# Gate sums of four chunks as triangular matmuls, clamp replaced by row sums, a first chunk in halves and constant matmuls, in a gated linear attention with a token-mixing block

## The chip, the cores and the metric

The kernel runs on one core of one Trainium2 chip. The metric is the device time of one execution in microseconds (us), the median of several runs: 340.54 us before, from 339.99 to 340.63 in three runs.

## The reference

Two stages, all in float32. The first is a recurrence over 768 tokens for 4 batches of 8 heads, with 48 values a head:

```
f = 1 / (1 + exp(-f_logit))
for t in range(S):
    state = f[:, :, t, :, None] * state + outer(k[:, :, t], v[:, :, t])
    y[:, :, t] = q[:, :, t] @ state
```

The second takes y as x with 384 channels a token:

```
theta = x @ w_theta
y = w_tok_r @ (x * cos(theta)) + w_tok_i @ (x * sin(theta))
u = x + y
out = u + maximum(u @ w_ch, 0)
```

## The kernel before, in words

The 768 tokens of a batch are cut into six chunks of 128, 24 chunks in all (m from 0 to 23). The eight heads lie as four pairs on the 128 partitions, so that a tile of q, k or f is 128 x 4 x 128, 256 KB.

*Gates of a chunk.* `gate_clamp` (L234) holds f at -44 or above, on VectorE or POOL. `gate_open` (L238) takes Exp and Ln on ScalarE, which gives minus the log of the gate. `gate_sum` (L244) sums it along the chunk's tokens with a scan on VectorE, where the constant tile carry begins each pair anew. `gate_exp` (L248) takes Exp of the negative sum into tile p, of which there is one buffer, and Exp of the sum in place of f. `gate_q` (L259) multiplies q by p, `gate_k` (L263) k by the held f tile. `gate_end` (L256) keeps the last column of p in `pes` on POOL.

*Attention of a chunk.* `att_keys` transposes k into psk, `att_ktok` copies it out, `att_state` (L314) forms k times v for both halves of the chunk, `att_scores` and `att_mask` (L300) the scores under the causal mask, `att_mid`, `att_new` and `att_fade` the state, `att_old` and `att_out` (L360) y, which `att_x` copies to x. v comes with a second copy whose heads are rolled.

*The second stage.* x is transposed (pxt) into ut; `angles` (L396) multiplies by w_theta into pth; `whole`, `settle`, `fold`, `trig` and `rotate` (L428) turn it into z = x cos, x sin; `products` (L447) sums z with the token weights over six chunks into pm; `add_u`, `split_uh`, `split_ul`, `channel` (pch) and `finish` do the rest. Batch 0 does this in float32; the later batches split each operand in a high and a low part in fp32r (`split_xh`, `split_xl`, `split_zh`, `split_zl`, `split_uh`, `split_ul`). The weights come as 64-bit floats; `decode_low`, `decode_high` and `decode_join` turn them into float32 (the steps d1, d2, d3), part by part: the parts 0 and 1 are w_theta, the next 12 the token weights.

*Order.* Nothing schedules the work but `ORDER` (L53): a list of steps, done from left to right, that puts each step's instructions behind the earlier ones of the same engine (L569). A letter after a slash moves the step to another engine (A ScalarE, D VectorE, P POOL). All loads and stores stand in one queue, SP's. A step is a name such as `gs` (gate_sum), `ge` (gate_exp), `gk`, `gq`, `ke` (att_keys), `up` (att_state) or `f0` (products for one third of the channels), and its n-th occurrence does the n-th chunk or piece.

*End.* `find_worst` (L500) makes a flag from `pes`; if it is set, a slow recurrence runs instead (it does not here). The last 128 x 3 x 384 tile is stored at L650, after the branch.

PSUM has two rings: two double banks "a", and four banks "b" for psk, pxt, pth, pm and pch.

Of the kernel before, what the change touches and what calls it, by code (L numbers as in the profile page):

```python
# [698 lines left out]
```

## Time and profile before

| | |
|---|---|
| median of 3 runs | 340.54 us |
| profiled execution | 340.03 us |
| its span, first to last instruction | 338.3 us |
| TensorE (PE) busy | 320.4 us, 95% |
| VectorE (DVE) busy | 251.6 us, 74% |
| ScalarE (ACT) busy | 188.7 us, 56% |
| POOL busy | 108.6 us, 32% |
| moved | 45.5 MB, 135 GB/s |

A busy share is that of the whole span, an average over stages that differ. PE is the matmuls and PEld the weight loads, which overlap them; the ends of matmuls are modelled. An f32 matmul shows as two records, a transpose as one. What matters is where an engine waits, and for whom.

### The profile page before, as it was taken

Reading aid. Unit: us, or ns where it says so; the run is one execution under the profiler, and the core shown is the slowest. Engines: PE = TensorE matmul, PEld = TensorE weight load, DVE = VectorE, ACT = ScalarE, POOL = GpSimd, SP = SyncE. Lnnn points to the kernel's source line nnn. Section 1 sums busy time; section 2 is a strip of 40 time slices with the busy share of each in tenths; the row PEclk is TensorE's granted clock in tenths of the full one; section 3 lists DMA queues with packets and bytes.
Section 4 is the critical chain, followed back from the end, with each engine's and each line's share of the span. In section 5 each row is a group of like instructions: output and inputs, shape, how many; then the busy total and the mean of one; then the engine's idle time right before and its main releaser. Section 6 shows DMA issues by size and latency. Waiting matters only on the chain. (4 is left out here: it accounts for less than half of the span.)

```text
span 338.3 us, 9998 instructions
## 1 busy us (share of the span) xinstructions
PE 320.4 (95%) x4320; PEld 283.2 (84%) x4320; DVE 251.6 (74%) x411; ACT 188.7 (56%) x308; POOL 108.6 (32%) x105
## 2 busy tenths in 40 slices
PE   0789999999999999999999999999999999999993
PEld 0676766776776789999999999999999999999992
DVE  5989999999999998898987857855437848534211
ACT  6787997995866755588476685244076114400010
POOL 3585152134418235701445423323212201300010
PEclk9999999999999999999999999999999999999998
DMA  7994994738761262374124320532121120000012
GB/s 256 382 401 168 317 372 151 249 114 323 244 224 30 64 230 82 91 233 141 33 85 149 122 79 2 187 114 84 40 73 48 47 73 27 0 2 0 11 60 78
DMA packets 21618, 45.54 MB, mean 135 GB/s; under 512 B 2368, under 2 KB 5440, under 8 KB 21568
## 3 DMA queue, kind: packets, MB, share of 16 engines
q1 hardware_dynamic: 21568, 44.84, 38.5%
q8 instruction: 36, 0.59, 0.7%
q14 instruction: 14, 0.11, 0.1%
HBM read 40.11 MB, written 4.72 MB: 133 GB/s over the span
## 5 line engine op out<-in xcount | busy, mean ns | idle before, releaser
L458 PE MATMUL pm<-wp,z 128*128 128x384 f32 x648 | 118.4, 337 | 0.0
L458 PEld LDWEIGHTS pm<-wp,z 128*128 128x128 f32 x648 | 112.4, 188 | 0.4
L458 PE MATMUL pm<-value,z 128*128 128x384 f32 x144 | 49.3, 487 | 0.0
L476 PE MATMUL pch<-uhl,wch 128*128 128x384 f32 x216 | 40.0, 337 | 0.0
L458 PEld LDWEIGHTS pm<-value,z 128*128 128x128 f32 x144 | 26.4, 190 | 15.2
L476 PEld LDWEIGHTS pch<-uhl,wch 128*128 128x128 f32 x216 | 37.4, 188 | 0.0
L469 POOL TENSOR_TENSOR uhl<-ut,uhl 128x384 fp32r<-128x384 f32 x13 | 14.2, 1094 | 67.0 <-ACT uhl L143 35.5
L236 POOL TENSOR_SCALAR f<-f 128x512 f32<-128x512 f32 x16 | 26.6, 1666 | 13.3 <-DMA f<-in_f_dram 12.5
L246 DVE TENSOR_TENSOR_SCAN f<-carry,f 128x512 f32<-128x512 f32 x24 | 29.8, 1246 | 1.4 <-ACT f L242 1.4
L257 POOL COPY pes<-p 128x4 f32<-128x4 f32 x24 | 10.5, 439 | 52.9 <-ACT p L253 52.9
L490 DVE SCALAR_TENSOR_TENSOR ut<-pch,ut 128x384 f32<-128x384 f32 x24 | 13.1, 550 | 18.8 <-PE pch L476 17.1
L308 PE MATMUL psk<-ident,k 128*128 128x128 f32 x96 | 16.9, 303 | 10.0 <-DVE k L266 10.0
L261 POOL TENSOR_TENSOR q<-q,p 128x512 f32<-128x512 f32 x12 | 17.3, 1446 | 23.1 <-ACT p L253 14.6
L462 DVE TENSOR_TENSOR ut<-pm,ut 128x384 f32<-128x384 f32 x24 | 13.0, 551 | 14.2 <-PE pm L458 14.2
L253 ACT ACTIVATE p<-f 128x512 f32<-128x512 f32 x24 | 15.1, 630 | 14.4 <-DVE f L246 6.8
L402 PE MATMUL pth<-wth,xh 128*128 128x384 f32 x108 | 23.0, 348 | 0.0
L308 PEld LDWEIGHTS psk<-ident,k 128*128 128x128 f32 x96 | 12.2, 153 | 12.3 <-issue 10.3
L435 DVE TENSOR_TENSOR w<-w,x 128x768 f32<-128x768 f32 x18 | 17.2, 962 | 6.3 <-ACT w L426 6.3
L143 ACT COPY x<-py 128x384 f32<-128x384 f32 x19 | 9.1, 478 | 22.5 <-PE py L361 22.1
L361 PEld LDWEIGHTS py<-v,sc 64*64 64x64 f32 x768 | 15.0, 140 | 7.4 <-issue 4.5
L143 ACT CAST uhl<-ut 128x384 fp32r<-128x384 f32 x7 | 3.6, 513 | 31.1 <-DVE ut L462 17.5
L266 DVE SCALAR_TENSOR_TENSOR k<-f,k 128x512 f32<-128x512 f32 x24 | 18.2, 758 | 1.8 <-ACT f L254 1.1
(83 smaller groups left out, 622.6 us busy)
## 6 DMA issues: line engine op xcount, KB each, us to landing
v<-in_v_dram SPq DMA_DIRECT2D x24, 384.0 KB, 4.3
f<-in_f_dram SPq DMA_DIRECT2D x24, 256.0 KB, 3.8
q<-in_q_dram SPq DMA_DIRECT2D x24, 256.0 KB, 4.1
k<-in_k_dram SPq DMA_DIRECT2D x24, 256.0 KB, 4.3
raw<-in_w_r_dram SPq DMA_DIRECT2D x12, 384.0 KB, 5.9
raw<-in_w_i_dram SPq DMA_DIRECT2D x12, 384.0 KB, 6.3
out_dram<-ut SPq DMA_DIRECT2D x21, 192.0 KB, 1.9
raw<-in_w_theta_dram SPq DMA_DIRECT2D x3, 384.0 KB, 6.4
```

The costliest lines, as they stand in the source:

```text
L236: on(nc.vector).tensor_scalar(ft, ft, F_MIN, None, op0=ALU.max)
L246: nc.vector.tensor_tensor_scan(fl, carry[:, pairs(h)].rearrange("p n t -> p (n t)"), fl, 0.0, ALU.mult, ALU.add)
L253: nc.scalar.activation(ps_[m][:, pairs(h)], ft, AF.Exp, scale=-1.0)
L261: on(nc.vector).tensor_tensor(qt, qt, ps_[m][:, pairs(h)], op=ALU.mult)
L266: nc.vector.scalar_tensor_tensor(kt, loaded["f", m][:, pairs(h)], E_TOP, kt, op0=ALU.min, op1=ALU.mult)
L308: nc.tensor.transpose(psks[m][:, p, :], loaded["k", m][:, p, :], ident)
L361: nc.tensor.matmul(out[HALF[t], j, p, :], scs[m][HALF[a], j, p, :], v2[HALF[a], t, p, :], start=(t == 0 and m % NC == 0 and p == 0), stop= ...
L402: nc.tensor.matmul(pths[m], l, r, start=(n == 0), stop=(n == len(ms) - 1))
L435: nc.vector.tensor_tensor(zs[m] if full else w, w, xs[m].unsqueeze(1).to_broadcast([P, 2, DM]), op=ALU.mult)
L458: nc.tensor.matmul(pms[g, d], l, r, start=(s == 0 and i == 0), stop=(s == NC - 1 and i == len(ms) - 1))
L469: on(nc.vector).tensor_tensor(us[g, d][:, 0], uts[g][:, d, :], us[g, d][:, 1], op=ALU.subtract)
L476: nc.tensor.matmul(pcs[g, d], l, r, start=(es[0] == 0 and n == 0), stop=(es[-1] == KD - 1 and n == len(ms) - 1))
```

## The change

- **The clamp goes.** `gate_open` writes, with its first Exp, the sum of each row into a column of `opened`; `find_worst` raises the flag where such a sum is above 1e18, too.
- **v** is loaded as three tiles of 192 columns instead of two of 384: 288 KB a chunk for 384.
- **Halves.** `CUT` is 1: chunk 0's loads and gates (f, k, q) are done in two halves of two pairs (the steps `hlf`, `hgo`, `hgs` and so on).
- **Sums as matmuls.** For the first four chunks (`SUMMED`) f is loaded with the tokens on the partitions (`ft`), and `gate_sum` is four f32 matmuls of 128x128 with the triangular tile `upto` into a bank of ring "b" instead of a scan. `gate_exp` reads that bank.
- **p and f change roles.** p holds Exp of the sum and meets k; the f tile holds Exp of its negative and meets q and `pes`.
- **Constant matmuls.** `keep_warm` (`wu`) multiplies the identity by a part of carry, into a bank nobody reads; there are 30.
- **New order.** `decode_high` can also be done on VectorE or POOL.

```diff
-CUT = 0
+CUT = 1
+SUMMED = 4
...
 ORDER = (
-    "lf gc lf gc go go gs lf gc/P lq lk lv gs ge gq gp go ge gk lw lk gs ke kt up gp sc lq gq/P d1 lw lq d2 gk ke",
+    "hlf wu wu wu hgo lf go lf go hlf hgo wu wu wu wu wu wu hgs lk wu wu wu gs gs ge wu lw hlq gk hgs hge hge d1",
+    "hlk hgk hgq/P wu hlq wu wu wu wu gp hlk hgk ke ke hgq d2 d3 lv kt ge up sc sa gp st sm/P lk kt lw d1 lv d2/P",
...
-    "f2 f2 ul so f2 cv cv c cv uh ul/P f2 v uh c c ul/P so c so so so rv cv cv cv",
+    "f2 f2 v uh ul/P f0 f0 uh/D ul c cv f1 f1 f1 f2 v v c cv f2 f2 gp fl c cv uh uh f2 f2 ul/P v uh ul c c ul/P c",
+    "rv wu wu so so so cv cv cv",
...
+    upto = const.tile([P, C], F32, tag="upto", name="upto")
+    nc.gpsimd.memset(upto, 1.0)
+    nc.gpsimd.affine_select(upto, upto, pattern=[[1, C]], compare_op=ALU.is_ge, fill=0.0, base=0, channel_multiplier=-1)
...
-    def gate_clamp(m, h=None):
-        ft = loaded["f", m][:, pairs(h)]
-        on(nc.vector).tensor_scalar(ft, ft, F_MIN, None, op0=ALU.max)
...
-        nc.scalar.activation(ft, ft, AF.Exp, scale=-1.0)
+        n = B * NC if h else m
+        nc.scalar.activation(ft, ft, AF.Exp, scale=-1.0, accum_out=opened[:, n:n + 1])
         nc.scalar.activation(ft, ft, AF.Ln, bias=1.0)
...
     def gate_sum(m, h=None):
+        if m < SUMMED:
+            if not h:
+                sums[m] = bank([P, NP, C], f"psum{m}")
+            for p in range(NP)[pairs(h)]:
+                nc.tensor.matmul(sums[m][:, p, :], loaded["f", m][:, p, :], upto, start=True, stop=True)
+            return
...
-        nc.scalar.activation(ps_[m][:, pairs(h)], ft, AF.Exp, scale=-1.0)
-        nc.scalar.activation(ft, ft, AF.Exp)
+        nc.scalar.activation(ps_[m][:, pairs(h)], src, AF.Exp)
+        nc.scalar.activation(ft, src, AF.Exp, scale=-1.0)
...
-        on(nc.vector).tensor_tensor(qt, qt, ps_[m][:, pairs(h)], op=ALU.mult)
+        on(nc.vector).tensor_tensor(qt, qt, loaded["f", m][:, pairs(h)], op=ALU.mult)
...
-        nc.vector.scalar_tensor_tensor(kt, loaded["f", m][:, pairs(h)], E_TOP, kt, op0=ALU.min, op1=ALU.mult)
+        nc.vector.scalar_tensor_tensor(kt, ps_[m][:, pairs(h)], E_TOP, kt, op0=ALU.min, op1=ALU.mult)
...
+    def keep_warm(n):
+
+        nc.tensor.matmul(bank([P, C], f"warm{n}"), ident, carry[:, 1], start=True, stop=True)
...
-        vs[m] = sb.tile([P, 2, DM], F32, tag="v", bufs=3, name=f"v{m}")
+        vs[m] = sb.tile([P, 3, NP * D], F32, tag="v", bufs=3, name=f"v{m}")
```

How the queues stand now, at three places. The first is TensorE's from its beginning to the first state update. Before, the whole of it was this:

```order
L308 MATMUL psk0_131<-ident_70,k0_109 128x128 x4
L322 MATMUL sk_138<-v0_111,ktok0_136 64x48 x16
L297 MATMUL sk0_156<-q0_107,k0_109 64x64 x16
L308 MATMUL psk1_184<-ident_70,k1_128 128x128 x4
L353 MATMUL py0_216<-mid0_191,q0_107 64x48 x8
```

Now it has constant matmuls (warm) and sums (psum) ahead of them; twelve of the constant ones and psum0's first half stand ahead of the first row here.

```order
L262 MATMUL psum1_141<-upto_79,f1_107 128x128 x4
L262 MATMUL psum2_146<-upto_79,f2_111 128x128 x4
L516 MATMUL warm12_154<-carry_67,ident_70 128x128
L262 MATMUL psum0_130<-upto_79,f0_96 128x128 x2
L516 MATMUL warm13_175<-carry_67,ident_70 128x128
...
L325 MATMUL psk0_189<-ident_70,k0_171 128x128 x4
L325 MATMUL psk1_194<-ident_70,k1_133 128x128 x4
L338 MATMUL sk_210<-v0_203,ktok0_205 64x48 x16
L314 MATMUL sk0_227<-q0_159,k0_171 64x64 x16
```

The transposes of chunk 1 (psk1) now stand right behind those of chunk 0 and ahead of chunk 0's update and scores.

The second is ScalarE's queue from the table load to the second chunk's exponentials; f0 is chunk 0, in halves of 256 columns.

```order
L237 ACT_TABLE_LOAD
L252 ACTIVATE f0_96,opened_87<-f0_96 128x256
L253 ACTIVATE f0_96<-f0_96 128x256
L252 ACTIVATE f1_107,opened_87<-f1_107 128x512
L253 ACTIVATE f1_107<-f1_107 128x512
L252 ACTIVATE f2_111,opened_87<-f2_111 128x512
L253 ACTIVATE f2_111<-f2_111 128x512
...
L273 ACTIVATE p1_151<-psum1_141 128x512
L274 ACTIVATE f1_107<-psum1_141 128x512
L273 ACTIVATE p0_164<-psum0_130 128x256
```

Before, chunks 0 and 1 were opened and chunk 0's exponentials came next; now three chunks are opened first, and chunk 1's exponentials come ahead of chunk 0's.

The third is VectorE's queue, from its first key gate on. Before:

```order
L246 SCALAR_TENSOR_TENSOR f1_95<-carry_67,f1_95 128x512
L261 TENSOR_TENSOR q0_107<-q0_107,p0_114 128x512
L266 SCALAR_TENSOR_TENSOR k0_109<-f0_92,k0_109 128x512
L246 SCALAR_TENSOR_TENSOR f2_104<-carry_67,f2_104 128x512
L182 TENSOR_SCALAR raw0_125<-raw0_125 128x768
L266 SCALAR_TENSOR_TENSOR k1_128<-f1_95,k1_128 128x512
```

And now:

```order
L286 SCALAR_TENSOR_TENSOR k1_133<-p1_151,k1_133 128x512
L190 TENSOR_SCALAR raw0_156<-raw0_156 128x768
L286 SCALAR_TENSOR_TENSOR k0_171<-p0_164,k0_171 128x256 x2
L281 TENSOR_TENSOR q0_159<-q0_159,f0_96 128x256
L203 SCALAR_TENSOR_TENSOR raw0_156<-raw0_156 128x768
L204 SCALAR_TENSOR_TENSOR value0_169<-raw0_156 128x768
L344 COPY mid0_244<-sk_210 128x192
```

The scans of these chunks are gone from it, and chunk 1's key gate stands ahead of chunk 0's two halves. In SP's queue the two loads of the first part of w_theta, 384 KB each, now stand ahead of q and k of chunk 0.

## Rows read from the trace of the kernel before

**Rows 1.** The page: busy time, share of the span and instructions, TensorE.

```profile
PE 320.4 (95%) x4320; PEld 283.2 (84%) x4320; DVE 251.6 (74%) x411; ACT 188.7 (56%) x308; POOL 108.6 (32%) x105
```

**Rows 2.** Waits of TensorE, the longest: us in total, times, longest us.

```profile
PE psk L308 <- DVE k L266: 10.0, 2, 9.6
```

**Rows 3.** Stretches: busy us by engine (instructions), granted clock, DMA share, GB/s.

```profile
0.00:10.00 10.00, 0.45 (x2) 0.48 (x3) 5.90 (x11) 6.82 (x11) 3.06 (x12) 1.00 0.81 278
10.00:20.00 10.00, 8.92 (x207) 7.58 (x210) 9.23 (x16) 7.77 (x14) 7.55 (x7) 1.00 1.02 384
20.00:30.00 10.00, 8.64 (x132) 6.26 (x125) 8.99 (x14) 8.54 (x15) 4.82 (x6) 1.00 0.89 340
30.00:40.00 10.00, 10.00 (x217) 6.62 (x215) 9.38 (x15) 7.98 (x14) 4.67 (x4) 1.00 0.66 201
40.00:60.00 20.00, 19.92 (x353) 13.30 (x356) 19.37 (x33) 16.45 (x26) 6.44 (x7) 1.00 0.73 264
```

**Rows 4.** Timeline at the end: start, duration, engine, line, operation.

```profile
331.63 1.67 DVE L490 SCALAR_TENSOR_TENSOR ut<-pch,ut 128x384 f32<-128x384 f32 x3 [3.08 <-PE pch L476]
333.43 0.39 SPq L650 DMA_DIRECT2D out_dram<-ut  x1
```

**Rows 5.** Timeline of TensorE's matmuls, six places between 9 and 59 us.

```profile
9.55 1.08 PE L308 MATMUL psk<-ident,k 128*128 128x128 f32 x4 [9.55 <-DVE k L266]
...
27.09 4.19 PE L402 MATMUL pth<-value,ut 128*128 128x384 f32 x6
...
32.66 0.60 PE L308 MATMUL psk<-ident,k 128*128 128x128 f32 x4
...
34.54 2.20 PE L402 MATMUL pth<-value,ut 128*128 128x384 f32 x6
...
41.83 1.46 PE L458 MATMUL pm<-value,z 128*128 128x384 f32 x4
...
56.01 2.74 PE L458 MATMUL pm<-value,z 128*128 128x384 f32 x8
```

**Rows 6.** Timeline of VectorE: the first key gate and the first z.

```profile
8.73 0.68 DVE L266 SCALAR_TENSOR_TENSOR k<-f,k 128x512 f32<-128x512 f32 x1
...
40.65 0.95 DVE L435 TENSOR_TENSOR z<-w,x 128x768 f32<-128x768 f32 x1
```

**Rows 7.** Timeline at the start: the clamps that wait for f's loads.

```profile
3.73 0.43 DVE L236 TENSOR_SCALAR f<-f 128x512 f32<-128x512 f32 x1 [2.14 <-DMA f<-in_f_dram]
...
6.41 1.61 POOL L236 TENSOR_SCALAR f<-f 128x512 f32<-128x512 f32 x1 [4.51 <-DMA f<-in_f_dram]
```

**Rows 8.** Groups by line and form: count, then busy us, mean ns, idle before.

```profile
L246 DVE TENSOR_TENSOR_SCAN f<-carry,f 128x512 f32<-128x512 f32 x24 | 29.8, 1246 | 1.4 <-ACT f L242 1.4
L236 POOL TENSOR_SCALAR f<-f 128x512 f32<-128x512 f32 x16 | 26.6, 1666 | 13.3 <-DMA f<-in_f_dram 12.5 <-DVE k L266 0.8
L241 ACT ACTIVATE f<-f 128x512 f32<-128x512 f32 x24 | 15.0, 627 | 4.0 <-DVE f L236 2.5 <-POOL f L236 1.4
L192 DVE SCALAR_TENSOR_TENSOR raw<-raw 128x768 int32<-128x768 int32 x14 | 13.7, 980 | 0.0
L393 POOL TENSOR_TENSOR xl<-ut,xh 128x384 fp32r<-128x384 f32 x10 | 10.8, 1084 | 24.1 <-DVE xh L143 12.3 <-ACT xh L143 11.8
L442 POOL TENSOR_TENSOR z<-w,z 128x768 fp32r<-128x768 f32 x5 | 9.6, 1925 | 24.2 <-ACT z L143 19.5 <-DVE z L143 4.8
L217 POOL TENSOR_TENSOR wp<-value,wp 128x768 fp32r<-128x768 f32 x5 | 11.1, 2213 | 0.5 <-DVE wp L143 0.5
L261 DVE TENSOR_TENSOR q<-q,p 128x512 f32<-128x512 f32 x12 | 8.6, 715 | 0.8 <-ACT p L253 0.8
L334 DVE TENSOR_TENSOR st<-sk,mid 128x192 f32<-128x192 f32 x20 | 7.0, 352 | 0.3
L143 DVE COPY ktok<-psk 128x512 f32<-128x512 f32 x7 | 4.8, 684 | 2.1 <-PE psk L308 2.0
L236 DVE TENSOR_SCALAR f<-f 128x512 f32<-128x512 f32 x8 | 3.5, 442 | 4.9 <-DMA f<-in_f_dram 4.9
```

More of the change, by code (lines that the diff above doesn't have):

```diff
@@ L35 @@
 A_MAX = 40.0
-F_MIN = -44.0
+G_TOP = 1e18
 E_MIN = 4.248354255291589e-18
@@ L98, in gla_moe_kernel @@
     f: bass.AP,
+    ft: bass.AP,
     v: bass.AP,
@@ L134, in gla_moe_kernel @@
     pes = const.tile([P, B * NC, NP], F32, tag="pes", name="pes")
+    opened = const.tile([P, B * NC + 1], F32, tag="opened", name="opened")
     here = [None]
@@ L186, in decode_high @@
         low, high = words(n)
-        nc.scalar.activation(high.bitcast(F32), high.bitcast(F32), AF.Copy, scale=2.0 ** -112)
+        if on(nc.scalar) is nc.scalar:
+            nc.scalar.activation(high.bitcast(F32), high.bitcast(F32), AF.Copy, scale=2.0 ** -112)
+        else:
+            on(nc.scalar).tensor_scalar(high.bitcast(F32), high.bitcast(F32), 2.0 ** -112, None, op0=ALU.mult)
     def decode_join(n):
@@ L228, in gla_moe_kernel, with bank @@
     loaded, ps_, phased, vs = {}, {}, {}, {}
+    def bank(shape, name):
+        return ps.tile(shape, F32, tag="b", bufs=4, name=name)
     def pairs(h):
         return slice(0, NP) if h is None else slice(2 * h, 2 * h + 2)
-    def gate_clamp(m, h=None):
-        ft = loaded["f", m][:, pairs(h)]
-        on(nc.vector).tensor_scalar(ft, ft, F_MIN, None, op0=ALU.max)
     def gate_open(m, h=None):
@@ L240, in gate_open @@
         gate_tables()
-        nc.scalar.activation(ft, ft, AF.Exp, scale=-1.0)
+        n = B * NC if h else m
+        nc.scalar.activation(ft, ft, AF.Exp, scale=-1.0, accum_out=opened[:, n:n + 1])
         nc.scalar.activation(ft, ft, AF.Ln, bias=1.0)
+    sums = {}
     def gate_sum(m, h=None):
+        if m < SUMMED:
[4 more added lines that the diff above has]
+            return
         fl = loaded["f", m][:, pairs(h)].rearrange("p n t -> p (n t)")
@@ L249, in gate_exp @@
         ft = loaded["f", m][:, pairs(h)]
+        src = sums[m][:, pairs(h)] if m < SUMMED else ft
         gate_tables()
@@ L252, in gate_exp @@
             ps_[m] = sb.tile([P, NP, C], F32, tag="p", bufs=1, name=f"p{m}")
[L253 to L254 removed]
+        nc.scalar.activation(ps_[m][:, pairs(h)], src, AF.Exp)
+        nc.scalar.activation(ft, src, AF.Exp, scale=-1.0)
     def gate_end(m):
[L257 removed]
+        nc.gpsimd.tensor_copy(pes[:, m, :], loaded["f", m][:, :, C - 1])
     def gate_q(m, h=None):
         qt = loaded["q", m][:, pairs(h)]
[L261 removed]
+        on(nc.vector).tensor_tensor(qt, qt, loaded["f", m][:, pairs(h)], op=ALU.mult)
     def gate_k(m, h=None):
         kt = loaded["k", m][:, pairs(h)]
[L266 removed]
+        nc.vector.scalar_tensor_tensor(kt, ps_[m][:, pairs(h)], E_TOP, kt, op0=ALU.min, op1=ALU.mult)
     pairs_, scs, psks, kts, mids, states, pys, xs, pxts = ({} for _ in range(9))
@@ L274, in last_chunk @@
         return m % NC == NC - 1
-    def bank(shape, name):
-        return ps.tile(shape, F32, tag="b", bufs=4, name=name)
     def two_banks(name):
@@ L319, in att_state @@
             for j in range(2):
-                h = 2 * p + j
                 for t in range(1 if last_chunk(m) else 2):
                     nc.tensor.matmul(out[HALF[j], t, p, :], kts[m][HALF[t], p, HALF[j]],
-                                     vs[m][HALF[t], 0, h * D:(h + 1) * D], start=True, stop=True)
+                                     vs[m][HALF[t], j, p * D:(p + 1) * D], start=True, stop=True)
     def att_mid(m):
@@ L356, in att_out @@
     def att_out(m):
-        out, v2 = y_of(m), vs[m][:, 1, :].rearrange("s (t p e) -> s t p e", t=2, p=NP)
+        out = y_of(m)
         for n, (p, t) in enumerate(OUT):
@@ L360, in att_out @@
                 j = a ^ t
-                nc.tensor.matmul(out[HALF[t], j, p, :], scs[m][HALF[a], j, p, :], v2[HALF[a], t, p, :],
+                nc.tensor.matmul(out[HALF[t], j, p, :], scs[m][HALF[a], j, p, :],
+                                 vs[m][HALF[a], 2 * j, p * D:(p + 1) * D],
                                  start=(t == 0 and m % NC == 0 and p == 0), stop=(p == NP - 1))
@@ L494, in store @@
         nc.sync.dma_start(out[b, d * P:(d + 1) * P, th * TH:(th + 1) * TH], uts[g][:, d, :])
+    def keep_warm(n):
+        nc.tensor.matmul(bank([P, C], f"warm{n}"), ident, carry[:, 1], start=True, stop=True)
     flag = const.tile([P, 1], I32, tag="flag", name="flag")
-    worst = const.tile([P, 2], F32, tag="worst", name="worst")
+    worst = const.tile([P, 3], F32, tag="worst", name="worst")
     def find_worst(_):
         nc.vector.tensor_reduce(worst[:, 0:1], pes, axis=AX.XY, op=ALU.min)
-        nc.vector.tensor_scalar(worst[:, 1:2], worst[:, 0:1], E_MIN, None, op0=ALU.is_lt)
+        nc.vector.tensor_reduce(worst[:, 1:2], opened, axis=AX.X, op=ALU.max)
+        nc.vector.tensor_scalar(worst[:, 0:1], worst[:, 0:1], E_MIN, None, op0=ALU.is_lt)
+        nc.vector.scalar_tensor_tensor(worst[:, 2:3], worst[:, 1:2], G_TOP, worst[:, 0:1], op0=ALU.is_gt, op1=ALU.add)
         pf = bank([P, 1], "pf")
-        nc.tensor.matmul(pf[:1, :], ones, worst[:, 1:2], start=True, stop=True)
+        nc.tensor.matmul(pf[:1, :], ones, worst[:, 2:3], start=True, stop=True)
         nc.vector.tensor_copy(flag[:1, :], pf[:1, :])
@@ L514, in go @@
                 loaded[nm, m] = sb.tile([P, NP, C], F32, tag=nm, bufs=bufs, name=f"{nm}{m}")
-            nc.sync.dma_start(loaded[nm, m][:, pairs(h)], src[m // NC, m % NC][:, pairs(h)])
+            rows = ft[m] if nm == "f" and m < SUMMED else src[m // NC, m % NC]
+            nc.sync.dma_start(loaded[nm, m][:, pairs(h)], rows[:, pairs(h)])
         return go
     def load_v(m):
-        vs[m] = sb.tile([P, 2, DM], F32, tag="v", bufs=3, name=f"v{m}")
+        vs[m] = sb.tile([P, 3, NP * D], F32, tag="v", bufs=3, name=f"v{m}")
         nc.sync.dma_start(vs[m], v[m // NC, m % NC])
@@ L542, in gla_moe_kernel @@
     by_halves = {
-        "lf": load("f", f, 3), "lk": load("k", k, 3), "lq": load("q", q, 3), "gc": gate_clamp, "go": gate_open,
+        "lf": load("f", f, 3), "lk": load("k", k, 3), "lq": load("q", q, 3), "go": gate_open,
         "gs": gate_sum, "ge": gate_exp, "gq": gate_q, "gk": gate_k,
@@ L559, in gla_moe_kernel @@
         "f0": piece(0), "f1": piece(1), "f2": piece(2), "v": group(add_u), "uh": group(split_uh), "ul": group(split_ul), "c": channels, "cv": group(finish),
-        "so": group(lambda g, d: store(g // NTH, g, d)), "fl": find_worst,
+        "so": group(lambda g, d: store(g // NTH, g, d)), "fl": find_worst, "wu": keep_warm,
     }
@@ L659, in rows @@
         return np.ascontiguousarray(t.transpose(0, 3, 2, 1, 4))
+    f = rows(inputs["f_logit"])
     v = np.asarray(inputs["v"])
@@ L664, in layout @@
     halves = v.transpose(0, 2, 1, 3).reshape(B, NC, 2, HF, NP, 2, D)
-    rolled = np.stack([np.stack([halves[:, :, t, :, :, a ^ t] for t in range(2)], axis=3) for a in range(2)], axis=2)
-    v2 = np.stack([halves.reshape(B, NC, C, DM), rolled.reshape(B, NC, C, DM)], axis=3)
-    v2 = np.ascontiguousarray(v2)
+    parts = [halves[..., 0, :], halves[..., 1, :], halves[:, :, ::-1, :, :, 1, :]]
+    v2 = np.ascontiguousarray(np.stack([a.reshape(B, NC, C, NP * D) for a in parts], axis=3))
     return {
@@ L670, in layout @@
         "k": rows(inputs["k"]),
-        "f": rows(inputs["f_logit"]),
+        "f": f,
+        "ft": np.ascontiguousarray(f.reshape(B * NC, P, NP, C)[:SUMMED].transpose(0, 3, 2, 1)),
         "v": v2,
```

1 line of the change is left out of this document (removed), and 65 rows, old and new, of the table ORDER.

## The prediction

> **What bounds the kernel now.** I read the page's busy line first: TensorE is busy for 320.4 of 338.3 us, with VectorE second at 251.6 [rows 1]. Then the waits of TensorE: one line carries 10.0 us, two waits for VectorE's first key gates [rows 2], and no other line of the list is much over 1 us. The stretches tell where that line lies: TensorE works 0.45 us of the first 10, 8.9 and 8.6 of the next two tens, then all of each stretch [rows 3]. So from about 31 us to its last matmul TensorE has no gap, and the run ends with a fixed tail: the last adds at 331.6, the last store's issue at 333.4, the end at 338.3 [rows 4]. A microsecond that TensorE gains before 31 us is a microsecond of the run; later it has none to gain, only to lose.
>
> The clock is the second thing. The stretches give a granted clock of 1.00 from the start [rows 3], but the same work says otherwise: six matmuls of 128x384 take 4.19 us at 27.1 and 2.20 at 34.5; four transposes take 1.08 at 9.6 and 0.60 at 32.7 [rows 5]. That is the ratio of the two levels, 1.2 and 2.4 GHz. TensorE is at the low one until the six matmuls that run from 27.1 to 31.2 without a gap, and at the high one after them. So 31 us hold an empty start of 9.5 us and some 21 us at half speed with gaps.
>
> One rule must be weighed here. At the high level the f32 product of 128x384 goes in pairs of records, eight in 2.74 us, one after the other without a wait [rows 5], although the weight loads fill only 13.3 us of 40 to 60 [rows 3]: the columns set the pace, not the loads. The Trainium skill (Perfetto Trace Analysis, Identifying the Most-Contended Engine) says that matmul busy time is a poor measure and that the busy share of weight loads is to be used. By that measure TensorE would be at two thirds from 30 to 115 us and VectorE, at 19.4 of 20, the bound; that is the first rival below. The rows of the eight products disagree with it for these matmuls.
>
> **The change part by part.** I follow it to one event: the start of the first product (pm), at 41.83 us before [rows 5]. It waits for z of chunk 0, which VectorE begins at 40.65 [rows 6].
>
> *The start.* The first f arrives at 3.73 us, and the third only at 6.41, since later loads share the engines [rows 7]. Now the queue brings half of chunk 0's f, then f1, f2 and the other half. With 128 KB less ahead I take f2 at 6.1. ScalarE then needs Exp and Ln for f2 (2 x 0.63 by the rows of 128x512 [rows 8]) and for the half (2 x 0.41, an estimate: 0.63 less half of its column part). That ends at 8.2. p1 follows to 8.85, and VectorE's first key gate, now that of chunk 1, starts at 8.9; before it was that of chunk 0, at 8.73 [rows 6]. So the start gains nothing. The clamp is off this path (0.43 us), but two chunks are opened ahead of the first gate.
>
> *Sums as matmuls.* Four chunks lose a scan of 1.25 us on VectorE (5.0 in all [rows 8]) and get four matmuls each. By the transposes' pace, 0.11 us a record and two records a plain f32 matmul, that is 0.9 us a chunk at the high level and 1.9 at the low. psum1 can start at 5.6 and is done by 7.5 even at the low level, before ScalarE is free for it at 8.2. psum0's second half is done by 9.2 at worst, and ScalarE wants it at 9.5. Hidden; 3.5 us of TensorE work fall into idle time.
>
> *Constant matmuls.* 30 of them, 0.22 us each high and 0.43 low. 27 stand in gaps ahead of the first product and are hidden if the gaps are there; one stands in the full stretch (+0.2); two stand behind the last product. They begin at about 1.7 us, when carry and the identity are set, and 12 of them with psum0's half fill TensorE until about 7.7 at the low level: a stretch without a gap, as the one ahead of the rise was before.
>
> *From the first key gate to z.* Before, VectorE goes from 8.73 to 40.65 with no more than 2.4 us idle in 10 to 40 [rows 3, 6], so this stretch is VectorE's list. I price both lists by the groups of lines, and a step without a row by the one of its size: 1.0 for 768 columns, 0.5 for 384. The new list drops the scans of f2 and f3 (2.5), two state fades (0.7), a weight split (1.0), two steps of decode and a shift for the fifth weight part (2.5), one 384-column step of the angles (0.5) and one chunk's middle and new state (0.7): -7.9. It gains two query gates (1.4), half a query gate and the second start of a halved key gate (0.6), a ktok copy (0.7), an x copy (0.5), a scale (0.5) and the scan of f6 (1.25): +5.0. Net -2.9 [rows 8]. Of the 2.4 us of idle time, part was for small matmuls at half speed; I take half back, 1.2, with bounds 0 and 2.4. So z starts at 8.9 + 31.9 - 2.9 - 1.2 = 36.7 and the first product at 37.7 to 37.8, 4.1 earlier. By then the new order has done one chunk's scores less (0.5 us). Lead: 3.6 us.
>
> TensorE can follow: up to there it has some 19 us of real work at the high level, 3.5 of sums and 6 of constants, 28.5 of the 36 us since 1.7.
>
> *From the first product on* TensorE's work is the same but for one constant matmul (-0.2). VectorE has 8 clamps (3.5 us) and 4 scans (5.0) less in all [rows 8], so it can keep up with a lead of 3.4. The 16 clamps of POOL (26.6 us) make room there for splits that VectorE gives away.
>
> *The rest.* Row sums: one more output on 24 Exp. No row shows its price; the bounds are 0 and 0.63, another whole ACTIVATE, and I take 0.1, nearer the first, as nothing is added but one column. Only two stand on the path: 0.2, within the rounding. ScalarE has 150 us idle. v at 288 instead of 384 KB takes 0.25 us off a load where the DMA share is about 1 [rows 3]; nothing waits for v there. The theta weights now go ahead of q0 and k0: 768 KB at 0.38 MB/us is 2 us later for k0, which puts it near 9; its gate comes at 10. Close, but covered. The store at the end is the same single one. The flag load moves ahead of three stores, beside some 5 us of matmuls.
>
> **Sum.** 338.3 - 3.6 + 0.2 = 334.9 us of span; the profiled execution took 340.03, 1.7 above its span and 0.5 below the median of 340.54. So **337.1 us** is forecast for the median.
>
> **The rivals.**
> 1. *VectorE was the bound up to 115 us* (the measure told above). For it: 97% busy from 40 to 60 [rows 3]. Against it: TensorE shows no waits there [rows 2]. Then the gain is what leaves VectorE, 8.5 us: 332.0.
> 2. *The clock stays low until the first long products.* For it: before, 17.6 us of TensorE work in 20 [rows 3], of transposes and small matmuls, did not raise it. Then each of three chunks in the chain keeps 0.5 us of slow transposes [rows 5] and, an estimate, as much again of slow updates, 3.1 in all, and the lead falls to 0.5: 340.2. The constants fill just those gaps, which speaks against it. The Trainium skill (TensorE: Matmul & The Clock Gate, Part 4) says that transposes do not count as busy for the clock; the rows of 10 to 27 us would agree, and the constants are no transposes.
> 3. *POOL holds up TensorE in the full stretch: slower.* The new order gives POOL 13 splits xl for 10 and 8 splits zl for 5; one takes 1.08 and 1.93 us there [rows 8], and it also gets five decode steps of some 2.2. TensorE's angles and products wait for these splits. If the 21 splits each end late by 0.3 us, 6.3 us are lost: 343.2. It turns from gain to loss at 0.17 us a split. Against it: POOL loses 26.6 us of clamps.
> 4. *The longer head eats the gain*: z waits for k0's later load, or for ScalarE, which opens three chunks ahead of the first gate; the lead is under 0.6 us: 340.5.
>
> **How the numbers follow.** Forecast 0.60 (its own bounds 334.5 to 339.3, from the idle time taken back and the start shifted by 1 us); rival 1 0.15; rival 2 0.10; rival 3 0.10; rival 4 0.05. About 0.2%, 0.7 us, is what a measurement here can tell. Faster: 0.60 + 0.15 + part of rival 2 = 0.80; same: the rest of rival 2 and rival 4, 0.10; slower 0.10. The range reaches from rival 1 nearly whole (332.2) to rivals 2 and 4 (340.8) and leaves out rival 3 and the far end of rival 1.
>
> **What would show it.** Right: the first matmuls at 1.7 us; transposes of chunk 0 at about 11.4 taking some 0.6 for four and not 1.08; the first product near 37.8; no TensorE waits from there on, and a last matmul near 329.3. Wrong: four transposes at 1.1 us (rival 2); waits of pth or pm for POOL's xl or z (rival 3); a first product after 41; or a lead that grows after 40 us (rival 1).

## The result: 343.94 us, slower by 1.3%

| | before | after |
|---|---|---|
| median (range, runs) | 340.53 us (339.99 to 340.63, 4) | 343.94 us (343.74 to 346.68, 4) |
| profiled execution | 340.03 us | 344.09 us |
| its span | 338.3 us | 342.2 us |

The ratio is 1.013 (95% interval 1.0095 to 1.0165). The forecast was 337.1, with a range that ended at 340.8. Of the runs below, 2, 12 and 14 have three, four and one executions over 1.5% above their fastest, which the ratios to before leave out; run 12's profiled execution is one of these.

The busy line of the page answers to [rows 1]:

```profile
PE 327.9 (96%) x4412; PEld 292.0 (85%) x4412; DVE 247.1 (72%) x399; ACT 194.2 (57%) x334; POOL 101.8 (30%) x106
```

VectorE and POOL have less to do than before, by 4.5 and 6.8 us; for VectorE the prediction counted 8.5. TensorE is busy for 7.5 us more, with constant matmuls and sums. ScalarE has 5.5 us more: its table loads, of 1.28 us each, are now 30 instead of 22. The stretches answer to [rows 3], in the same columns (PE, PEld, DVE, ACT, POOL, clock, DMA share, GB/s):

```profile
0.00:10.00 10.00, 8.26 (x51) 8.29 (x52) 1.25 (x5) 6.79 (x15) 1.62 (x11) 1.00 0.80 253
10.00:20.00 10.00, 8.42 (x184) 7.19 (x183) 8.50 (x16) 7.82 (x16) 4.49 (x7) 1.00 0.90 296
20.00:30.00 10.00, 8.84 (x251) 7.18 (x250) 8.39 (x14) 8.37 (x17) 1.46 (x2) 1.00 0.94 329
30.00:40.00 10.00, 8.57 (x181) 6.10 (x179) 9.93 (x14) 7.97 (x15) 3.95 (x4) 1.00 0.64 213
40.00:60.00 20.00, 19.18 (x292) 12.65 (x287) 18.37 (x32) 16.25 (x28) 6.41 (x6) 1.00 0.78 267
```

Read the last two first. TensorE was full from 30 us on before; now it stands still for 1.4 of 10 us and 0.8 of the next 20. VectorE is idle for 1.5 and 1.6 us in the tens from 10 to 30, and the loads bring 296 GB/s from 10 to 20 for 384 before.

The start, on TensorE, ScalarE and VectorE, from the timeline:

```profile
1.74 4.18 PE L516 MATMUL warm<-carry,ident 128*128 128x128 f32 x18 [1.74 <-POOL causal L131]
...
7.50 1.95 PE L262 MATMUL psum<-upto,f 128*128 128x128 f32 x16
...
8.59 0.60 ACT L273 ACTIVATE p<-psum 128x512 f32<-128x512 f32 x1 [0.70 <-PE psum L262]
...
9.22 0.69 DVE L286 SCALAR_TENSOR_TENSOR k<-p,k 128x512 f32<-128x512 f32 x1 [7.62 <-ACT p L273]
...
12.05 0.68 PE L325 MATMUL psk<-ident,k 128*128 128x128 f32 x4 [0.62 <-DVE k L286]
...
39.35 0.95 DVE L452 TENSOR_TENSOR z<-w,x 128x768 f32<-128x768 f32 x1
...
40.44 2.82 PE L475 MATMUL pm<-value,z 128*128 128x384 f32 x8
```

The constant matmuls start where they should. Four transposes take 0.68 us, where those of [rows 5] took 1.08: the clock is at its high level, and the trace's clock record has it rise at 7.1 us and stay. ScalarE waits 0.70 us for the first sums it needs, and the first key gate comes at 9.22 (forecast 8.9), z at 39.35 (36.7), the first product at 40.44 (37.8; before 41.83). So the head gained 1.4 us of the 4.1 that were forecast. And then that gain goes. What TensorE waited for (us in total, times, longest), and the end of the timeline:

```profile
PE psk L325 <- DVE k L286: 1.8, 2, 1.2
...
PE sk L338 <- ACT ktok L151: 1.7, 3, 0.8
PE sk L338 <- DVE ktok L151: 0.9, 1, 0.9
```

```profile
331.49 4.84 PE L493 MATMUL pch<-uhl,wch 128*128 128x384 f32 x27
...
335.33 1.67 DVE L507 SCALAR_TENSOR_TENSOR ut<-pch,ut 128x384 f32<-128x384 f32 x3 [2.62 <-PE pch L493]
...
337.13 0.39 SPq L674 DMA_DIRECT2D out_dram<-ut  x1
```

The tail is as long as in [rows 4]: the last adds 3.70 us later than before, the last issue 3.70, the end 3.9. All the loss lies ahead of the tail.

**A measure for the rest: the lead at equal work.** I add up what TensorE has behind it at a moment (transposes, state matmuls, scores, angles, products, each kind by its duration at the high clock), and look up when the kernel before, in the trace of the groups above, had as much behind it. Constant matmuls and sums count nothing. Here are all the runs; "loss" is the lead at 35 us less that at 330.

| run | order | p, f | median us | lead at 35 | at 90 | at 330 | loss |
|---|---|---|---|---|---|---|---|
| after | new | new | 343.94 | 0.8 | -1.5 | -3.7 | 4.5 |
| 1 no constants | new | new | 342.38 | 2.4 | -0.4 | -2.0 | 4.4 |
| 2 before + 27 constants | old | old | 339.04 | 2.1 | 2.2 | 2.0 | 0.1 |
| 3 parts, old order | old | new | 348.34 | -1.0 | -8.3 | -8.2 | 7.2 |
| 4 as 3, scans | old | new | 344.22 | 1.9 | -4.0 | -3.7 | 5.5 |
| 5 decode on ScalarE | new | new | 344.64 | 2.2 | -0.4 | -2.4 | 4.6 |
| 6 split moved | new | new | 342.99 | 3.3 | -0.3 | -2.2 | 5.5 |
| 7 copies early | new | new | 344.17 | 2.4 | -1.2 | -2.9 | 5.3 |
| 8 before, no clamp | old | old | 341.34 | -1.0 | -2.4 | -2.1 | 1.1 |
| 9 before + VectorE work | old | old | 341.25 | 2.1 | 1.4 | 1.0 | 1.1 |
| 10 lighter list | new | new | 342.99 | 0.3 | -3.4 | -4.5 | 4.9 |
| 11 lighter and early | new | new | 341.06 | 4.4 | 1.1 | -0.1 | 4.5 |
| 12 scans, new order | new | new | 343.94 | 0.1 | -4.0 | -6.3 | 6.4 |
| 13 load and copy placed | new | new | 342.62 | 2.4 | -0.7 | -2.0 | 4.4 |
| 14 before, clock held | old | old | 341.33 | 2.0 | 1.6 | 0.8 | 1.1 |
| 15 as 13 + constants | new | new | 344.38 | 2.9 | -3.4 | -6.2 | 9.2 |
| 16 after - 3 scans | new | new | 343.13 | 2.8 | 0.5 | -1.5 | 4.3 |
| 17 before - 3 scans | old | old | 340.34 | -0.6 | -0.3 | -1.0 | 0.4 |
| 18 after + VectorE work | new | new | 345.45 | 1.6 | -1.9 | -4.0 | 5.6 |

The leads are those of one profiled execution each, the medians of 4 to 12 runs, so a row's lead and its median need not fit, and a difference of half a microsecond between two leads says little. The last column is the finding: it does not follow the head.

### The profile page after: what moved, and what is told of

Its sections match the earlier page's. It is cut to its first block, busy times and chain, and to the rows that moved or that the text cites. A ratio compares the mean times of both kernels' runs of the same rounds, so it can differ in the third digit from the quotient of the medians.

```text
span 342.2 us, 10248 instructions
## 1 busy us (share of the span) xinstructions
PE 327.9 (96%) x4412; PEld 292.0 (85%) x4412; DVE 247.1 (72%) x399; ACT 194.2 (57%) x334; POOL 101.8 (30%) x106
## 4 chain that ended last, share of the span: by engine, by line
PE 73%; DVE 14%; issue 4%; DMA 4%; ACT 2%; SPq 1%; POOL 1%; DVEq 0%; ACTq 0%; POOLq 0%
PE pm L475 39%; PE pch L493 9%; PE pth L419 8%; PE py L377 3%; PE py L369 3%; PE sk L314 2%; PE sk L338 2%; PE pxt L388 2%; DVE k L286 2%; PE psk L325 2%; DMA raw<-in_w_theta_dram 2%; DMA raw<-in_w_i_dram 1%; DVE raw L203 1%; DVE raw L190 1%; DVE f L265 1%
## 5 line engine op out<-in xcount | busy, mean ns | idle before, releaser
L486 POOL TENSOR_TENSOR uhl<-ut,uhl 128x384 fp32r<-128x384 f32 x15 | 17.0, 1138 | 58.4 <-ACT uhl L151 45.5
L151 ACT CAST uhl<-ut 128x384 fp32r<-128x384 f32 x15 | 7.7, 512 | 46.3 <-DVE ut L479 39.1
L410 POOL TENSOR_TENSOR xl<-ut,xh 128x384 fp32r<-128x384 f32 x13 | 13.9, 1070 | 55.4 <-ACT xh L151 31.6
L265 DVE TENSOR_TENSOR_SCAN f<-carry,f 128x512 f32<-128x512 f32 x20 | 24.6, 1238 | 4.2 <-ACT f L253 4.0
L459 POOL TENSOR_TENSOR z<-w,z 128x768 fp32r<-128x768 f32 x8 | 15.5, 1940 | 35.5 <-ACT z L151 18.7
L286 DVE SCALAR_TENSOR_TENSOR k<-p,k 128x512 f32<-128x512 f32 (+1 forms) x25 | 19.6, 785 | 8.0 <-ACT p L273 7.9
L281 POOL TENSOR_TENSOR q<-q,f 128x512 f32<-128x512 f32 (+1 forms) x11 | 15.1, 1374 | 33.6 <-ACT f L274 28.2
L419 PE MATMUL pth<-wth,xh 128*128 128x384 f32 x108 | 23.2, 350 | 0.1
L452 DVE TENSOR_TENSOR w<-w,x 128x768 f32<-128x768 f32 x18 | 19.0, 1058 | 6.0 <-ACT w L443 5.9
L273 ACT ACTIVATE p<-f 128x512 f32<-128x512 f32 x20 | 12.7, 633 | 15.0 <-DVE f L265 12.7
L419 PEld LDWEIGHTS pth<-wth,xh 128*128 128x128 f32 x108 | 18.6, 188 | 1.4 <-DVE w L430 0.4
```

Source lines behind the costliest of these rows:

```text
L265: nc.vector.tensor_tensor_scan(fl, carry[:, pairs(h)].rearrange("p n t -> p (n t)"), fl, 0.0, ALU.mult, ALU.add)
L281: on(nc.vector).tensor_tensor(qt, qt, loaded["f", m][:, pairs(h)], op=ALU.mult)
L286: nc.vector.scalar_tensor_tensor(kt, ps_[m][:, pairs(h)], E_TOP, kt, op0=ALU.min, op1=ALU.mult)
L419: nc.tensor.matmul(pths[m], l, r, start=(n == 0), stop=(n == len(ms) - 1))
L452: nc.vector.tensor_tensor(zs[m] if full else w, w, xs[m].unsqueeze(1).to_broadcast([P, 2, DM]), op=ALU.mult)
L459: on(nc.vector).tensor_tensor(zs[m][:, 0], ws[m], zs[m][:, 1], op=ALU.subtract)
```

## The experiments

**1. Without the constant matmuls** (`wu` struck from the new order).

> The changed kernel without its 30 constant matmuls. In the changed kernel four transposes took 0.6 us already at 12 us, and its first product began at 40.4 us; TensorE then lost some 7 us in waits and ended 4 us later than before. Theory A (the new table asks for operands too early from 30 us on; the raised clock is real and worth something): the transposes at 12 us take 1.1 us again, the first product moves to 42 to 44, the run takes 345.5 to 348. Theory B (VectorE, over 97% busy to 115 us in both kernels, eats any lead that TensorE has at 40 us): the first product moves as well, but the run stays at 343.5 to 344.5. If the sums alone keep the clock up, nothing changes at all.

Measured: 342.38 us (342.28 to 343.45), ratio to before 1.0102 (1.0061 to 1.0142). It is not slower than the changed kernel, and its first product comes at 38.97, earlier and not later, so neither theory's range fits. By the trace's clock record the sums alone raise the clock at 9.9 us; it falls from 13.3 to 16.7 and then stays up. The constants are not what carries the clock, and the loss behind 35 us is the same without them.

**2. The constants alone, in the kernel before** (27 `wu` put into the old order).

> The kernel before with 27 constant matmuls put into TensorE's gaps ahead of its first products, 20 of them ahead of the first transposes; nothing else. Theory A: the clock is up by 8 us, the first product starts at 38.5 to 40.5 instead of 41.8, nothing waits later, and the run takes 337.5 to 339.5. Theory B: the first product is as early, and the lead is waited away by 115 us: 340 to 341.

Measured: 339.04 us (338.1 to 344.03), ratio 0.9996 (0.9958 to 1.0034). Stretches of its trace, 10 to 30 us:

```profile
10.00:20.00 10.00, 8.34 (x234) 7.02 (x236) 9.37 (x16) 7.86 (x15) 7.38 (x7) 0.83 1.05 400
20.00:30.00 10.00, 8.54 (x186) 6.01 (x177) 9.50 (x15) 8.29 (x15) 7.13 (x6) 0.83 0.87 331
```

The granted clock of 0.83 tells that it fell twice for part of a stretch. The lead of 2.1 us at 35 is kept to the end, which speaks against VectorE eating up any lead. In the median nothing is won; the kernel before reaches the same lead by itself in the profiled execution of run 9.

**3 and 4. The parts of the change in the old order.** The old table without `gc`, chunk 0 whole, 27 constants, all else as changed; in the fourth run also `SUMMED = 0`, so scans for all chunks.

> All parts of the change except its table: the old table without the clamp steps, chunk 0 whole, the sums of four chunks as matmuls, row sums, v in three tiles, p and f with their roles changed, and 27 constant matmuls in TensorE's gaps ahead of the first products. Theory A: this takes the gain without the loss, 334 to 338. Theory B: VectorE has 8 clamps and 4 scans less, so part of the lead gets through: 336 to 339. If a part itself (the sums in ring b, the row sums, p's one buffer) is what slows the changed kernel, it stays above 341.

> As the third, but all 24 chunks keep their scans (no sums on TensorE). The difference between the two is the worth of the sums as matmuls in the old table. Theory A: 336 to 339, the sums worth 1 to 2 us. Theory B: 338 to 340. If the sums cost more at the start than they give, this one is the faster of the two.

Measured: 348.34 us (347.1 to 350.6), ratio 1.0278 (1.0219 to 1.0338); and 344.22 us (343.65 to 345.02), ratio 1.0154 (1.0114 to 1.0195). The sums as matmuls cost 2.9 us of lead at 35 in this order, in the profiled pair. Both lose the rest in one place, at 70 to 80 us. The timeline of run 4 there, with VectorE, SP's queue and TensorE, then from its view of the transfers the load of v (the last number is us from issue to landing), and what SP waited for from 60 to 76 us:

```profile
69.36 0.68 DVE L278 TENSOR_TENSOR q<-q,f 128x512 f32<-128x512 f32 x1
...
70.11 0.33 SPq L536 DMA_DIRECT2D f<-in_f_dram  x1
70.49 0.42 SPq L541 DMA_DIRECT2D v<-in_v_dram  x1
...
73.90 1.09 PE L335 MATMUL sk<-v,ktok 64*64 64x48 f32 x32 [4.19 <-ACT f L249]
```

```profile
v<-in_v_dram SPq DMA_DIRECT2D x1, 288.0 KB, 3.3
```

```profile
SPq L536 <- DVE q L278: 8.6, 1, 8.6
```

Read upwards: the state matmuls start at 73.90, after 4.19 us without work. The wait is put down to ScalarE's f, but v was issued at 70.49 and took 3.3: it landed at 73.8. It stood in SP's queue behind a load of f, and that one could go only at 70.11, when the query gate had let go of f's buffer. **That is the swap of p and f**: before, the key gate frees an f buffer; now the query gate does, and the last-column copy to `pes`, which is POOL's. Run 3 waits 4.0 us at the same step, there put down to the load of v itself. The clock adds to the loss: by the clock record it is low behind this stall, from 74.0 to 77.4 us in run 4 and from 76.2 to 83.1 in run 3.

**8. The kernel before without clamps**, with the row sums, constants as in 2, p and f in their old roles.

> The kernel before, in its own order, with 27 constant matmuls and without the clamps (row sums instead); p and f keep their roles, v its two tiles. Against the run with the constants alone (338.1 in its profile) the theory that the swap of p and f made the 4 us stall at 74 us of the fourth run (loads of f and v queued behind the query gate) says: no such stall, 337.5 to 338.8. If the stall came from the missing clamps or the row sums: again 341.5 to 344.

Measured: 341.34 us (340.04 to 342.35), ratio 1.0047 (1.0024 to 1.0071). The stall is gone: v is issued well ahead, and the same state matmuls follow without a gap.

```profile
67.00 0.42 SPq L526 DMA_DIRECT2D v<-in_v_dram  x1
...
73.82 0.67 PE L322 MATMUL sk<-v,ktok 64*64 64x48 f32 x32
```

The lead is -2.4 at 90 and -2.1 at 330 us. The time missed its forecast all the same, in the head: v of chunk 1 landed 1.89 us late, and the clock was low from 11.4 to 21.6 and again from 35.3 to 38.7. Why this head is slower than run 2's stays open. So the swap, or v in three tiles, which runs 3 and 4 have too, makes the stall of 4 us in the old order; no run separates the two, and that the swap does it is what the rows say.

**5. POOL's decode steps of 51, 61 and 68 us back on ScalarE** (`d2/P` to `d2`).

> The changed kernel with three of POOL's five decode steps of 768 columns (51.4, 61.1 and 68.3 us) back on ScalarE. Theory S (stalls: TensorE loses single waits for copies that come late, and each one removed comes back whole at the end): VectorE's join and shift beside POOL's step at 68.3 go back from 1.54 and 1.04 to 0.96 and 0.55, the sines start 1 us earlier, TensorE's wait for ktok at 75 (0.8 to 1.0) goes, and the run takes 342.7 to 343.2. Theory R (rate: from 35 us VectorE's list as a whole sets the pace): the wait goes and another takes its place, 343.6 to 344.2.

Measured: 344.64 us (342.87 to 345.76), ratio 1.0164 (1.011 to 1.0219). VectorE's join and shift went back to 0.96 and 0.55. But ScalarE, with the decode in its own queue, was now late with p, for which VectorE waited 0.82, and the wait of TensorE's weight loads for the keys near 75 shrank only from 0.9 to 0.5, while that near 49 grew by 0.2. The median is no better.

**6. The first theta split from POOL to VectorE's idle place** (`d5/P` struck, `d5` ahead of the scan at 49 us). First the place in the changed kernel's timeline, POOL and VectorE:

```profile
31.82 1.82 POOL L228 TENSOR_TENSOR wth<-value,wth 128x768 fp32r<-128x768 f32 x1
...
32.01 2.18 DVE L286 SCALAR_TENSOR_TENSOR k<-p,k 128x512 f32<-128x512 f32 x1
```

> The changed kernel with the split of the first theta weights (POOL, 31.8 us, 1.8 us) moved to VectorE, to its idle place at 47.6 to 49.1. Theory S: the key gate of chunk 4 takes 0.7 instead of 2.18, TensorE's wait of 1.2 before its transposes at 34.2 is gone, the lead at 35 us is 2 instead of 0.8, and the run takes 342.4 to 343.0. Theory R: the lead at 35 us grows as well, but is gone by 90 us: 343.6 to 344.2.

Measured: 342.99 us (341.54 to 345.76), ratio 1.0115 (1.0038 to 1.0192). The same gate and the transposes behind it:

```profile
30.81 0.68 DVE L283 SCALAR_TENSOR_TENSOR k<-p,k 128x512 f32<-128x512 f32 x1
...
32.08 0.66 PE L322 MATMUL psk<-ident,k 128*128 128x128 f32 x4
```

Right on the spot: 0.68 for 2.18, and no wait of TensorE (it was 1.2). The lead at 35 us is 3.3, for 1.6 to 2.8 in runs 5, 7, 16 and 18, which have the changed kernel's steps up to there. By 90 us it is -0.3, as theory R had it; the median lies in theory S's range, but its interval covers both.

**7. Two key copies early.**

> The changed kernel with two copies of the transposed keys placed earlier in their queues: the one of 50 us ahead of two gate openings on ScalarE, the one of 88 us ahead of a split and a shift on VectorE. Theory S: the two waits of TensorE (0.94 and 1.06) go and the run takes 341.9 to 342.4. Theory R: 343.4 to 344.2.

Measured: 344.17 us (343.0 to 344.34), ratio 1.013 (1.0075 to 1.0185). The two waits went; waits for x (0.9 twice), a sum (0.8) and an angle (0.8) took their place. Theory S falls.

**9 and 17. More and less VectorE work in the kernel before.**

```diff
+    def extra(n):
+        nc.vector.scalar_tensor_tensor(carry, carry, E_TOP, carry, op0=ALU.min, op1=ALU.mult)
```

> The kernel before with four more VectorE operations of 128x512 (about 0.68 us each, 2.7 in all, on the constant tile carry, which they leave as it is), each just ahead of the joins of a weight part, between 58 and 85 us. Nothing waits for them. Theory V (from the first product to about 90 us VectorE's list sets the pace: it is busy 46.7 of 48.2 us there): TensorE loses 1.3 to 2.7 us by 90 us and keeps the loss: 341.8 to 343.2 against 340.5. Theory S (only single late copies cost; VectorE has slack against TensorE between them): under 0.5 us lost, 340 to 341.

> The kernel before without the scans of the same three chunks (50.7, 51.8 and 62.3 us): 3.7 us less on VectorE. If VectorE is not the bound of the kernel before, where TensorE has no waits there: the same time within 0.4 us, and the lead at 95 us equal to that at 40. If it is: up to 3.7 us faster.

Measured: 341.25 us (339.39 to 342.84), ratio 1.0049 (1.002 to 1.0077), with the lead falling from 2.4 to 1.0 between 80 and 95 us; and 340.34 us (338.73 to 341.44), ratio 1.0007 (0.9975 to 1.0038). So less VectorE work does not speed up the kernel before, and of 2.7 us more it hides some 1.3 and loses 1.4.

**10 and 11. A lighter VectorE list in the new order** (four `tn/D` to `tn`, one `d4/D` to `d4`; in 11 also the edits of 6 and 7).

> The changed kernel without its constant matmuls (342.4) and with five steps of VectorE between 40 and 90 us back on ScalarE: four roundings of the angles and one high part of a weight, 2.7 us of VectorE's list. Theory V: lead against before at 90 us +1.0 to +2.3 instead of -0.4, and 339.8 to 341.2. Theory S: the waits for the copied keys at 49, 75 and 88 us stay as long, ScalarE being fuller makes them longer if anything: 342.2 to 343.5.

> As the one before, and the two copies of the keys placed early (49 and 88 us) and the split of the first theta weights on VectorE at 47 us. Theory V: the split adds 0.95 to VectorE's list and the early copies none: 339.5 to 341.5, not better than the one before by over 0.7. Theory S: 340.0 to 341.0, 2 us better than the one before.

Measured: 342.99 us (342.51 to 344.6), ratio 1.0092 (1.0056 to 1.0128); and 341.06 us (339.97 to 342.94), ratio 1.0046 (1.0016 to 1.0075), the fastest of the new order. VectorE is busy for some 47.5 us of the stretch of equal work (41.8 to 90 us before) in either, 1.4 less than in run 1, and the loss stays 4.9 and 4.5: theory V falls for run 10. That 11 beats 10 by 1.9 us is what theory S said, but what 11 has over 10 is the head, 4.1 us at 35 in the profiled pair: in 10 the clock fell from 24.9 to 31.7.

**12. Scans for all chunks in the new order.**

> The changed kernel without its constant matmuls and with scans on VectorE for all chunks (no sums as matmuls), in the new order: 5 us more on VectorE ahead of 36 us. If VectorE's list sets the pace from the first gate to 90 us: 2.5 to 5 us later throughout, 345 to 347.5. If the head waits for loads and for ScalarE and VectorE has room there: the lead at 40 us falls by under 2 us, 342.4 to 344.

Measured: 343.94 us (341.26 to 346.91), ratio 1.0078 (1.0046 to 1.0109). The profiled one, near the upper end, has the clock rise only at 27.0, and low again from 37.2 to 40.7. Without the sums' matmuls TensorE is idle at the start, and that changes the clock along with VectorE's list. The run doesn't price the sums by themselves.

**13 and 15. A load of k ahead of two of f, a key copy off ScalarE's queue**, on top of 11; in 15 with the 30 constants.

> The eleventh run's kernel (341.06, without constant matmuls) with two more steps placed: the load of k that VectorE waited 1.58 us for at 50 us now ahead of two f loads in SP's queue, and the copy of the keys at 72 us on VectorE instead of behind a table load and two sines on ScalarE. Theory S (order of single steps): VectorE's wait for k goes, TensorE's 1.23 at 52 and 0.3 to 0.9 of its 1.24 at 72 go, 339.3 to 340.6. Theory V (VectorE's list as a whole): the copy adds 0.7 to VectorE's list, 341 to 342.

> The first of these three with the changed kernel's 30 constant matmuls back. If these cost TensorE time in a full stretch (as the first run's 1.5 us said): 0.5 to 1.5 us slower than without. If they only keep the clock from falling in some runs: the same or up to 1 us faster, and the runs spread less.

Measured: 342.62 us (340.5 to 344.69), ratio 1.0081 (1.005 to 1.0113); 344.38 us (342.79 to 347.46), ratio 1.0127 (1.0093 to 1.0161). What the weight loads waited for, in run 11 and then in run 13 (total, times, longest):

```profile
PEld pm L472 <- DVE z L449: 1.4, 2, 1.0
PEld sk L335 <- ACT ktok L148: 1.1, 1, 1.1
```

```profile
PEld pm L472 <- DVE z L449: 1.6, 3, 0.8
...
PEld pm L472 <- DVE ut L476: 0.9, 1, 0.9
```

The wait for ScalarE's copy went, and products waited for sums and for z instead. The loss is 4.4, and the median is above both theories' ranges. In run 15 the clock also fell from 90.5 to 93.9, after a wait of TensorE at 88; its 9.2 is not to be compared.

**14. The kernel before with its clock held** (48 constants in its gaps).

> The kernel before with 48 constant matmuls instead of the 27 of the second run, in the gaps where its clock fell (8 to 11 and 18 to 25 us). If the head before is slow by its clock: the clock is up from about 5 us on, the first product at 39.0 or earlier, 336.5 to 338.5. If gates and loads set the head: no better than the second run's 338.1 to 339.1.

Measured: 341.33 us (337.55 to 343.75), ratio 1.0027 (0.9993 to 1.006). The clock was up from 7.4 us to the end, and the lead at 35 us is 2.0, as in run 2. A clock that is up throughout brings no more than that of run 2, which fell twice; what is left of this head is not the clock's. The median is no better, and five of twelve runs lie below 339.3, the others above 340.7.

**16 and 18. Less and more VectorE work in the changed kernel.** The scans of three chunks left out, as in 17; the four operations of 9 put in.

```diff
     def gate_sum(m, h=None):
...
+        if m in (7, 8, 9):
+            return
         fl = loaded["f", m][:, pairs(h)].rearrange("p n t -> p (n t)")
```

> The changed kernel without the scans of chunks 7, 8 and 9 (the sums of their gates are left out): 3.7 us less on VectorE between 49 and 79 us, nothing more on any other engine. If VectorE's list sets the pace there: the lead against before at 90 us rises by 2 to 3.7 (from -1.5), the copy of the keys at 88 us is no longer waited for by 1 us, and the run takes 340.3 to 342. If single late copies by ScalarE and the loads set it: under 0.8 us better.

> The changed kernel with the four more VectorE operations of the ninth run (2.7 us in all), between 60 and 80 us. If VectorE's list sets the pace there, the whole of it is lost (the kernel before had 1.3 us of room and lost 1.44): lead at 90 us -3.5 to -4.5 instead of -1.5, 345.9 to 346.9. If not: as in the kernel before or less, 344 to 345.4.

Measured: 343.13 us (342.12 to 345.26), ratio 1.0094 (1.0062 to 1.0126); 345.45 us (344.59 to 347.09), ratio 1.0164 (1.0089 to 1.024). With 3.7 us taken from VectorE the wait at 88 us went, and that of the weight loads at 49 grew from 0.8 to 1.5. From the chain of waits of run 16, start and duration:

```profile
39.91 1.68 POOL q L283
41.59 0.61 POOL pes L279
...
42.21 4.18 DMA f<-in_f_dram
...
46.47 0.73 ACT f L252 x2
...
49.04 0.58 ACT ktok L151
```

POOL's query gate and the copy to `pes` end at 42.2; only then can f's load go. It takes 4.18, ScalarE opens two chunks with it, and then copies the keys that TensorE stands for. The lead at 90 us is 2.0 more than the changed kernel's, but it had that at 35 us already, ahead of the edit. Neither theory on VectorE holds: 3.7 us less brought no shorter loss (4.3), 2.7 us more cost about 1.1.

## Why the prediction was wrong

Of the 7 us between forecast and profile, 2.8 lie ahead of 35 us and 4.3 behind.

*The clock and the constants* went as told: first matmuls at 1.7 us, high level from 7.1. Rival 2 did not come. But run 1 shows that the constants were not needed, and runs 2 and 14 that the clock was not all that the head waited for.

*"psum1 can start at 5.6 and is done by 7.5"*, so hidden: it started at 7.50, and ScalarE waited 0.70 us for it. The prediction's own next step has twelve constant matmuls fill TensorE until about 7.7, and these stand ahead of psum1 in the queue. In run 1, without them, ScalarE takes psum1 at 7.51 with no wait, and the first key gate starts at 8.14.

*"So z starts at 8.9 + 31.9 - 2.9 - 1.2 = 36.7"*: z came at 39.35. The step priced VectorE's list by durations of instructions alone. One key gate took 2.18 instead of 0.68 beside POOL's split, which run 6 undid. And VectorE was idle for 3.2 us from 10 to 40, for loads and for its partners, where I had left it 1.2. The rest differs from execution to execution: the lead at 35 us is 1.6 to 2.8 in runs 5, 7, 16 and 18, with the same steps up to there, 0.8 in the changed kernel's own trace. So how far the head missed is in part chance; in run 11 the first product comes at 37.09, ahead of the forecast.

*"VectorE can keep up with a lead of 3.4"* is the step that failed most. It compared totals: 8.5 us less for VectorE in the whole kernel, so no wait of TensorE from the first product on. By the page VectorE has only 4.5 less, and TensorE lost 4.5 us behind 35, in run 11 too, which has the head that was forecast. Against the step stands the chain of waits of the changed kernel, which runs through VectorE from 60.6 to 88.6 us. Its pieces, start and duration:

```profile
60.64 0.56 DVE x L151
...
71.26 0.59 DVE k L286
71.85 0.47 DVE w L430
72.35 0.52 ACT w L435
72.89 1.28 ACT L442
...
87.89 0.61 DVE ktok L151
88.55 0.68 PE sk L338 x32
```

The fifth weight part, two roundings and a split, which the prediction took off the head's list, stand in this stretch now. In the stretch of equal work (41.8 to 90 us before, 41.0 to 91.8 after) VectorE is busy 47.1 and 48.3 us: longer, in spite of the clamps and scans that it lost. Run 9 shows how little room it had. But its total is not the cause by itself: runs 10, 11 and 16 took work off it in this stretch, and the loss stayed at 4.3 to 4.9. What failed is the step from a total to "no waits": TensorE waits for single copies, sums and z that come late in the queues. At 72.9 a table load of ScalarE's 30 stands ahead of two sines and of the copied keys that TensorE waits for.

The other chain is the swap's. In the changed kernel's timeline, from POOL by way of SP's queue and ScalarE to TensorE:

```profile
41.59 1.73 POOL L281 TENSOR_TENSOR q<-q,f 128x512 f32<-128x512 f32 x1
43.27 1.11 POOL L277 COPY pes<-f 128x4 f32<-128x4 f32 x2
...
43.94 0.80 SPq L539 DMA_DIRECT2D f<-in_f_dram  x2
...
47.58 0.63 ACT L252 ACTIVATE f<-f 128x512 f32<-128x512 f32 x1 [2.51 <-DMA f<-in_f_dram]
...
50.15 0.57 ACT L151 COPY ktok<-psk 128x512 f32<-128x512 f32 x1
...
50.77 0.68 PE L338 MATMUL sk<-v,ktok 64*64 64x48 f32 x32 [0.70 <-ACT ktok L151]
```

The prediction has no line on the swap of p and f: I read it as a renaming. It changes which step frees f's buffer, and with it when SP may go on. SP stood at this load from 39.2 us; the key gates of chunks 4 and 5, whose f buffers it and the next one take, had ended at 34.2 and 37.0. The wait of TensorE at the chain's end is 0.70 us; what the loads queued behind it cost is not shown. In SP's waits the key gate of before (34.1 us, 9 times, for these loads) gives way to this:

```profile
SPq L539 <- POOL pes L277: 16.9, 2, 12.2
SPq L539 <- DVE q L281: 11.5, 7, 4.2
```

*What is shown and what is open.* Shown: the loss of 4.3 to 5.6 us behind the head stands in ten kernels of the new order (12 and 15, with fallen clocks, lose more), whatever single wait or VectorE step was changed; every kernel with the old roles of p and f, in the old order, loses 0.1 to 1.1; and in the old order the new roles lose over 4 us, at a wait that the rows lead back to f's buffer. The stall of 4 us is shown there alone. Not shown: how much of the new order's loss is the swap's and how much the order's. The new order with the old roles would tell; it was not tried.

*Rivals.* Rival 3 was nearest in its number (343.2), with a mechanism that did not come: TensorE waits for no xl or zl. POOL does act, by the query gate ahead of f's load and by holding up instructions of VectorE that run beside its own. Rival 4 came in part: ScalarE and the loads did make the head longer, but 1.4 us of its gain stayed. Rival 1 falls with run 17: less VectorE work didn't speed up the kernel before. That is also the answer on the rule of the Trainium skill (Perfetto Trace Analysis, Identifying the Most-Contended Engine) that I weighed: by the weight loads' share VectorE would have been the bound there, and it was not.

No version beats the kernel before by more than the measurement can tell: run 2 equals it, and run 11, the best of the new order, is 0.5% above it.
